# A PSUM tile read by four operations, and the same tile copied out first: one step of a fused forward and backward kernel

## The chip, the cores and the metric

The kernel runs on one core of a Trainium2 chip. The metric is the device time of one execution in microseconds (us): the median of several runs. The engines are PE (TensorE, matrix products out of SBUF into PSUM), DVE (VectorE), ACT (ScalarE), POOL (GpSimd) and SP (SyncE, which here issues DMA transfers). Each engine runs its own instructions in order and waits for others by semaphores.

## The reference

The program computes one block of a speech model (attention beside a gated convolution, merged by a second convolution) and the gradients of all its inputs. B = 2, T = 4000, D = 144, everything in bfloat16. What matters here is the attention and its backward pass:

```
xa  = layernorm(x)
q, k, v = split(xa @ w_qkv)
p   = softmax(q @ k.T / sqrt(D))
attn = p @ v;  glob = attn @ w_att_out
...
out = x + (m + conv(m)) @ w_merge        # m = [glob, loc]
outputs: out and the gradients of x and of all seven weights, for the given grad_out
```

## The kernel before, in words

The projections are folded into small weight products, so that attention works on the normalized input xa itself. For each batch element, `phase_att` goes over 32 tiles of 125 query rows (line 1234, `for t in range(NB + 1)`); the same instructions carry the forward pass and the backward pass of the attention. For tile i:

- `quad` (L1044 to 1056): PE makes scores S and their gradients dP against all 4000 keys, in pieces of 2 x 500 columns. Two PSUM buffers "ps" of 2 x 500 columns hold these pieces in turn; each 500 columns take a main matmul (L1049) and one for the 16 input columns left over (L1055).
- `S_min` (L1072, 1074): DVE copies a score piece, negated, into Pbuf and takes the row minimum; `P_exp` (L1079): ACT turns it into exponentials in place. They stay unnormalized: the row sum comes later, from Y.
- `PdP`: ACT casts a dP piece into Sbuf (L1090) and DVE multiplies it by P (L1092), or DVE does both (L1087).
- `P_tr` (L1082) and `st_half` (L1253): DMA transposes of Pbuf into PT and of Sbuf into ST, issued by SP.
- `Y_half` (L1094 to 1122): Y = P xa, 32 matmuls over the 32 key blocks (L1100), 125 x 145, whose column 144 is the row sum, since xa_aug has a column of ones. Then rl = 1 / row sum (L1106, DVE); dj (L1109, DVE) sums Y times the tile's gradient rows qb into delta; nd = -delta rl (L1111, DVE); yn = Y rl (L1113, ACT), stored to DRAM by SP (L1114); ty = Y nd (L1116, ACT), a term for Z; and QBs (L1118 to 1122, four POOL operations), the rescaled rows that X uses.
- `Z_half` (L1132 to 1144): Z = (P dP) xa by another 32 matmuls (L1138); zn = Z rl + ty (L1142, DVE).
- `X_group` (L1163 to 1183): the key side of the backward pass, X, by matmuls of Sbuf and Pbuf against QBs (L1177), added into acc by DVE (L1183).

Y and Z share one PSUM tile "yz", [125, 2, 145] in f32: one buffer (bufs=1, line 1096 or 1134) holds Z of tile i in its second half and Y of tile i + 1 in its first half. The next such tile is Z of tile i + 1 and Y of tile i + 2, so Z of tile i + 1 can start only when every reader of Y of tile i + 1 is done.

Between the attention steps stand the units of the convolution branch (`local_units`, L421 to 663). Nothing of the order is left to chance: class `Planner` (L666 to 968) takes the program of a phase as a graph, gives each instruction an estimated cost by engine, size and memory (`cost`, L713), starts on each engine the earliest instruction of the program that is ready and has its buffers, and fixes the resulting order on all engines. A new instruction is thus a new node of the graph, and orders elsewhere may change too.

The small tiles come from the pool `small` (L980), with 4 buffers where no number is given.

Of the kernel before, what the change touches and what calls it, by code (L numbers as in the profile page):

```python
# [8 lines left out]
F32 = mybir.dt.float32  # L9
# [7 lines left out]
PB = 125  # L17
# [953 lines left out]
def phase_att(k, W, b, S, A, M, head=None):  # L971
    nc, tc = k.nc, k.tc
# [5 lines left out]
    with ExitStack() as es:  # L978
        ab = es.enter_context(tc.tile_pool(name="att_buf%d" % b, bufs=1, side="left", reuse_waits="tile"))
        small = es.enter_context(tc.tile_pool(name="att_small%d" % b, bufs=4, side="left", reuse_waits="tile"))  # L980
# [113 lines left out]
        def Y_half(i, h):  # L1094
            if h == 0 and i not in YZ:
                yz = ps_yz.tile([PB, 2, 145], F32, tag="yz")
                YZ[i] = yz
            Y = YZ[i][:, 0, :]
            for j in range(16 * h, 16 * h + 16):
                nc.tensor.matmul(Y, PT[0:PB, j, 0:PB], xaa[:, j, 0:D + 1], start=(j == 0), stop=(j == NB - 1))  # L1100
            if h == 0:
                return
            qb = QB.pop(i)
            rl = small.tile([PB, 1], F32, tag="rl")
            RL[i] = rl
            nc.vector.reciprocal(rl[:], Y[:, 144:145])  # L1106
            delta = small.tile([PB, 1], F32, tag="delta")
            dj = small.tile([PB, D], BF, tag="dj", bufs=1)
            nc.vector.scalar_tensor_tensor(dj[:], Y[:, 0:D], rl[:], qb[:, 1, 0:D], op0=ALU.mult, op1=ALU.mult, accum_out=delta[:])  # L1109
            nd = small.tile([PB, 1], F32, tag="nd")  # L1110
            nc.vector.scalar_tensor_tensor(nd[:], delta[:], -1.0, rl[:], op0=ALU.mult, op1=ALU.mult)  # L1111
            yn = small.tile([PB, D], BF, tag="yn", bufs=2)
            nc.scalar.activation(yn[:], Y[:, 0:D], ACT.Copy, scale=rl[:])  # L1113
            nc.sync.dma_start(S.Yn_d[:, i, :], yn[:])  # L1114
            ty = small.tile([PB, D], F32, tag="ty", bufs=2)
            nc.scalar.activation(ty[:], Y[:, 0:D], ACT.Copy, scale=nd[:])  # L1116
            TY[i] = ty
            nc.gpsimd.tensor_scalar(QBs[:, i % NPB, 0, :], qb[:, 0, 0:D], rl[:], 1.0, op0=ALU.mult, op1=ALU.mult)  # L1118
            g0, g1 = (small.tile([PB, D], F32, tag=n_, bufs=1, name=n_) for n_ in ("g0", "g1"))
            nc.gpsimd.tensor_scalar(g1[:], qb[:, 1, 0:D], rl[:], 1.0, op0=ALU.mult, op1=ALU.mult)  # L1120
            nc.gpsimd.tensor_scalar(g0[:], qb[:, 0, 0:D], nd[:], 1.0, op0=ALU.mult, op1=ALU.mult)
            nc.gpsimd.tensor_tensor(QBs[:, i % NPB, 1, :], g0[:], g1[:], op=ALU.add)  # L1122
# [111 lines left out]
        for t in range(NB + 1):  # L1234
# [31 lines left out]
            if head is not None and t < 2:  # L1266
                for s in range(8):
                    for f in steps[8 * t + s]:
                        f()
                    if s < 4:  # L1270
                        S_min(t, s, quad(S_work(t, s), t > 0)[0])
                        if t == 0 and s == 3:
                            for c2 in range(4):
                                P_exp(0, c2)
                    elif t:
                        PdP(0, s - 4, quad(dP_work(0, s - 4))[0], s % 2 == 1)
                for h in range(2 * t):
                    st_half(h)
                    Y_half(0, h)
                if t == 0:  # L1280
                    P_tr(0)
                continue
# [40 lines left out]
            if t < NB:  # L1323
                products(3)
                for h in range(2):
                    if ok(t - 1):
                        Y_half(t - 1, h)
# [11 lines left out]
        for h in range(2):  # L1339
            Y_half(NB - 1, h)  # L1340
# [631 lines left out]
```

## Time and profile before

| | |
|---|---|
| median of 3 runs | 1405.17 us (1404.89 to 1405.4) |
| span of the profiled execution, first to last instruction | 1401.5 us |
| own time of the profiled execution | not listed apart from the span |
| mean granted clock of PE | 0.976 |
| busy: PE, weight loads, DVE, ACT, POOL | 1298.7, 1069.5, 1055.4, 830.5, 541.5 us |
| ACT yn (L1113), ty (L1116), mean of 64 | 372, 375 ns |
| DVE rl (L1106), dj (L1109), nd (L1111), mean of 64 | 161, 361, 180 ns |
| POOL QBs and helpers (L1118, L1120, L1121, L1122), mean of 64 | 397, 414, 401, 508 ns |

The span has a head (0 to 60 us), the attention phase of the first batch element (60 to 660), its merge (to about 760), the attention phase of the second (760 to 1300) and its merge and the final weight gradients. A line of groups or of a timeline names the source line, the engine, the operation and "out<-in" with tile names; "[0.95 <-ACT ty L1116]" means that the engine sat idle for 0.95 us before it and that this ended when ACT finished the instruction of line 1116. In an answer on waits the numbers are the total, the count and the longest.

### The profile page before, as it was taken

The numbers are of one execution on the slowest core, as the hardware profiler recorded it, in microseconds if no ns is written. First come the engines' busy times: TensorE is split into PE (matmuls) and PEld (weight loads), VectorE is DVE, ScalarE is ACT, GpSimd is POOL, SyncE is SP. The second block draws the span as 40 slices with busy tenths as digits, with TensorE's granted clock in tenths as the row PEclk, the third lists the DMA queues.
The fourth block names the chain that finished last, engine by engine and source line by source line (L and its number), as shares of the span: only waits on it lengthen the run. The fifth ranks groups of instructions, "written<-read, shape, count | busy, mean of one in ns | idle before, by whom it ended". The sixth has DMA issues, their size and how long they took to land.

```text
span 1401.5 us, 39725 instructions
## 1 busy us (share of the span) xinstructions
PE 1298.7 (93%) x16254; PEld 1069.5 (76%) x16254; DVE 1055.4 (75%) x2815; ACT 830.5 (59%) x1387; POOL 541.5 (39%) x1087
## 2 busy tenths in 40 slices
PE   5879999999999999998787999999999999999898
PEld 3557877778877877888775778788887787787887
DVE  7368878788887878767737888788888887876564
ACT  4656666666666665553626666666766665565371
POOL 7453333334333333347514334343443433334420
PEclk8899999999999999999998999999999999999999
DMA  4367657757776776785225877767776766866512
GB/s 116 77 106 138 121 107 127 143 108 125 123 125 128 128 128 124 119 175 145 75 54 97 149 129 128 129 127 131 129 135 123 135 126 115 145 122 129 160 42 72
DMA packets 553637, 168.60 MB, mean 120 GB/s; under 512 B 536431, under 2 KB 548353, under 8 KB 553412
## 3 DMA queue, kind: packets, MB, share of 16 engines
q1 hardware_dynamic: 547818, 153.74, 59.5%
q0 software_dynamic: 5088, 12.11, 3.3%
q8 instruction: 127, 2.08, 0.6%
q14 instruction: 56, 0.46, 0.1%
q10 hardware_dynamic: 548, 0.21, 0.1%
HBM read 21.04 MB, written 14.12 MB: 25 GB/s over the span
## 4 chain that ended last, share of the span: by engine, by line
PE 42%; DVE 7%; DMA 7%; ACT 4%; POOL 3%; issue 2%; DVEq 0%; SPq 0%; POOLq 0%; ACTq 0%
PE X L1177 9%; PE ps L1049 7%; PE yz L1138 5%; PE yz L1100 5%; DMA PT<-Pbuf 4%; PE ps L1055 3%; PE po L1525 2%; ACT Pbuf L1079 1%; DMA go_h<-in_grad_out_dram 1%; DVE t L1551 1%; DVE Pbuf L1072 1%; PE pd L564 1%; DMA ST<-Sbuf 1%; DVE acc L1183 1%; PE pc L549 1%
## 5 line engine op out<-in xcount | busy, mean ns | idle before, releaser
L1072 DVE TENSOR_SCALAR_CACHE_REDUCE Pbuf<-ps 125x1000 bf16<-125x1000 f32 x256 | 306.5, 1198 | 119.5 <-PE ps L1055 115.5
L1079 ACT ACTIVATE Pbuf<-Pbuf,nm 125x1000 bf16<-125x1000 bf16 x256 | 283.2, 1135 | 125.8 <-DVE nm L1074 125.7
L1177 PE MATMUL X<-QBs,Sbuf 125*125 125x144 bf16 x2048 | 304.0, 230 | 7.0 <-DVE acc L1183 3.2
L1177 PE MATMUL X<-QBs,Pbuf 125*125 125x144 bf16 x2048 | 300.1, 228 | 4.7 <-POOL QBs L1122 4.7
L1049 PE MATMUL ps<-xaT_m,qt 128*125 128x500 bf16 x1024 | 270.2, 382 | 13.4 <-DVE Pbuf L1072 4.7
L1177 PEld LDWEIGHTS <-Sbuf 125*125 125x125 bf16 x2048 | 264.8, 139 | 20.2 <-issue 20.0
L1177 PEld LDWEIGHTS <-Pbuf 125*125 125x125 bf16 x2048 | 265.6, 139 | 8.5 <-issue 8.2
L1090 ACT CAST Sbuf<-ps 125x1000 bf16<-125x1000 f32 x189 | 187.8, 994 | 139.8 <-PE ps L1055 139.3
L1183 DVE TENSOR_TENSOR acc<-X,acc 125x432 f32<-125x432 f32 x372 | 202.6, 551 | 55.9 <-PE X L1177 53.6
L1138 PE MATMUL yz<-xa_aug,ST 125*125 125x144 bf16 x2048 | 150.1, 229 | 19.4 <-ACT ty L1116 18.3
L1049 PEld LDWEIGHTS <-qt 128*125 128x125 bf16 x1024 | 124.0, 139 | 56.9 <-issue 18.1
L1138 PEld LDWEIGHTS <-ST 125*125 125x125 bf16 x2048 | 141.1, 139 | 26.0 <-issue 24.5
L1100 PE MATMUL yz<-xa_aug,PT 125*125 125x145 bf16 x2048 | 146.4, 229 | 7.3 <-DMA PT<-Pbuf 7.0
L1092 DVE TENSOR_TENSOR Sbuf<-Sbuf,Pbuf 125x1024 bf16<-125x1024 bf16 x189 | 134.3, 711 | 22.4 <-ACT Sbuf L1090 22.1
L1100 PEld LDWEIGHTS <-PT 125*125 125x125 bf16 x2048 | 136.9, 138 | 15.2 <-DMA PT<-Pbuf 10.4
L1055 PEld LDWEIGHTS <-qt 16*125 16x125 bf16 x1024 | 37.1, 129 | 102.9 <-issue 102.9
L1055 PE MATMUL ps<-XR,qt 16*125 16x500 bf16 x1016 | 113.0, 424 | 0.0
L1087 DVE TENSOR_TENSOR Sbuf<-ps,Pbuf 125x1000 bf16<-125x1000 f32 x67 | 80.0, 1194 | 4.6 <-PE ps L1055 2.8
L1118 POOL TENSOR_SCALAR QBs<-qb,rl 125x144 bf16<-125x144 bf16 x64 | 25.4, 397 | 136.9 <-DVE rl L1106 133.2
L597 POOL TENSOR_TENSOR A_dwc<-l_fl,A_dwc 128x512 f32<-128x512 f32 (+2 forms) x48 | 35.5, 740 | 104.3 <-ACT l_fl L596 104.2
L574 POOL TENSOR_SCALAR l_w<-gd,nc,c 125x144 f32<-125x144 bf16 x64 | 30.6, 485 | 87.1 <-DVE nm L1074 44.7
L1152 ACT COPY zt<-pt 128x250 bf16<-128x250 bf16 x64 | 23.7, 370 | 66.6 <-PE pt L1150 66.4
(557 smaller groups left out, 2562.5 us busy)
## 6 DMA issues: line engine op xcount, KB each, us to landing
Yn_d<-yn SPq DMA_DIRECT2D x64, 35.2 KB
Zn_d<-zn SPq DMA_DIRECT2D x64, 35.2 KB
ug_d<-ugr SPq DMA_DIRECT2D x32, 70.3 KB
xo<-in_x_dram SPq DMA_DIRECT2D x16, 140.6 KB
out_dram<-dxo SPq DMA_DIRECT2D x16, 140.6 KB
go_h<-in_grad_out_dram POOLq DMA_DIRECT2D x4, 504.0 KB, 6.7
Zn<-Zn_d SPq DMA_DIRECT2D x4, 504.0 KB
ST<-Sbuf SPq DMA_TRANSPOSE x124
```

The costliest lines, as they stand in the source:

```text
L597: nc.gpsimd.tensor_tensor(acc, fl[0:rows, 0:n], acc, op=ALU.add)
L1049: mm = nc.tensor.matmul(pp[r // 2][:, r % 2, 0:CH], QT[i][:, 3 * h, :], xaTm[:, c * CH:(c + 1) * CH], start=True, stop=False)
L1055: nc.tensor.matmul(pp[r // 2][:, r % 2, 0:CH], QT[i][rs, 1 + (q // 2 + h) % 2, :], xr, start=False, stop=True)
L1072: nc.vector.tensor_scalar(pv(Pbuf, i % NPB, c2), src, -1.0, 3.0e38, op0=ALU.mult, op1=ALU.min, accum_out=NM[i][:, c2:c2 + 1])
L1079: nc.scalar.activation(v, v, ACT.Exp, bias=NM[i][:, 4:5], scale=-1.0)
L1087: nc.vector.tensor_tensor(pv(Sbuf, i % NDB, c2), src, pv(Pbuf, i % NPB, c2), op=ALU.mult)
L1090: nc.scalar.copy(pv(Sbuf, i % NDB, c2), src)
L1092: nc.vector.tensor_tensor(sc, sc, pchunk(i % NPB, c2), op=ALU.mult)
L1100: nc.tensor.matmul(Y, PT[0:PB, j, 0:PB], xaa[:, j, 0:D + 1], start=(j == 0), stop=(j == NB - 1))
L1138: nc.tensor.matmul(Z, ST[0:PB, j, 0:PB], xaa[:, j, 0:D], start=(j == 0), stop=(j == NB - 1))
L1177: nc.tensor.matmul(X[:, jj, :], l, r, start=(n_ == 0), stop=(n_ == len(ops) - 1))
L1183: nc.vector.tensor_tensor(av, X[:, 0:nj, :], av, op=ALU.add)
```

## The change

After the last Y matmul of a tile, ACT copies all 145 columns of Y out of PSUM into a new SBUF tile ys (f32, two buffers), and the name Y then stands for that copy: rl, dj, yn and ty read ys. Nothing else differs in the source.

```
--- before.py
+++ after.py
@@ -1101,6 +1101,9 @@
             if h == 0:
                 return
             qb = QB.pop(i)
+            ys = small.tile([PB, 145], F32, tag="ys", bufs=2)
+            nc.scalar.copy(ys[:], Y)
+            Y = ys
             rl = small.tile([PB, 1], F32, tag="rl")
             RL[i] = rl
             nc.vector.reciprocal(rl[:], Y[:, 144:145])
```

Lines after 1103 of the old program are three lines further down in the new one: yn, L1113 before, is L1116 after, and ty, L1116 before, is L1119 after.

More of the change, by code (lines that the diff above doesn't have):

```diff
@@ L1103, in Y_half @@
             qb = QB.pop(i)
+            ys = small.tile([PB, 145], F32, tag="ys", bufs=2)
+            nc.scalar.copy(ys[:], Y)
+            Y = ys
             rl = small.tile([PB, 1], F32, tag="rl")
```

## The prediction

> **What bounds the kernel now.** I read the busy shares first, then the stages, then what TensorE (PE) waits for in the two long stages, then one such wait instruction by instruction.
>
> The page's first part gives PE 93% of the span, VectorE (DVE) 75%, ScalarE (ACT) 59%. The stretches of time show where this holds (columns: length, then PE, weight loads, DVE, ACT and POOL busy, granted clock, DMA share, GB/s):
>
> ```profile
> 60.00:660.00 600.00, 566.73 (x7106) 466.84 (x7107) 465.57 (x1209) 361.29 (x578) 243.66 (x494) 0.98 0.70 128
> ...
> 760.00:1300.00 540.00, 521.20 (x6580) 426.42 (x6580) 434.11 (x1076) 339.86 (x545) 204.39 (x413) 1.00 0.73 132
> ```
>
> These are the attention phases of the two batch elements. PE is idle for 33.3 us of the first and 18.8 us of the second; no other engine is above 80%. PE runs its instructions in a fixed order, so nearly every idle microsecond of PE there is time lost. The waits of PE in the two stretches name the causes:
>
> ```profile
> PE yz L1138 <- ACT ty L1116: 12.4, 12, 2.3
> PE yz L1100 <- DMA PT<-Pbuf: 2.7, 6, 0.8
> PE X L1177 <- DVE acc L1183: 2.5, 5, 0.9
> ...
> PE X L1177 <- POOL QBs L1122: 2.0, 3, 1.6
> ```
>
> ```profile
> PE yz L1138 <- ACT ty L1116: 6.0, 5, 2.6
> PE yz L1100 <- DMA PT<-Pbuf: 4.3, 5, 1.1
> ...
> PE X L1177 <- POOL QBs L1122: 1.1, 1, 1.1
> ```
>
> The reader sees one leading cause: the matmuls of Z (L1138) wait 12.4 + 6.0 = 18.3 us (17 times; unrounded) for the ACT operation that makes ty (L1116), the last reader of Y in the one PSUM buffer that Y and Z share. One such wait, with start, length, engine and line:
>
> ```profile
> 217.31 0.80 PE L1100 MATMUL yz<-xa_aug,PT 125*125 125x145 bf16 x10
> ...
> 218.14 0.17 DVE L1106 RECIPROCAL rl<-yz 125x1 f32<-125x1 f32 x1 [0.55 <-PE yz L1100]
> ...
> 218.35 0.37 DVE L1109 SCALAR_TENSOR_TENSOR dj<-yz,rl,qb 125x144 bf16<-125x144 f32 x1
> 218.41 0.38 POOL L1118 TENSOR_SCALAR QBs<-qb,rl 125x144 bf16<-125x144 bf16 x1 [2.98 <-DVE rl L1106]
> ...
> 218.75 0.38 ACT L1113 ACTIVATE yn<-yz,rl 125x144 bf16<-125x144 f32 x1
> 218.75 0.20 DVE L1111 SCALAR_TENSOR_TENSOR nd<-delta,rl 125x1 f32<-125x1 f32 x1
> ...
> 219.67 0.39 ACT L1116 ACTIVATE ty<-yz,nd 125x144 f32<-125x144 f32 x1
> ...
> 220.10 1.30 PE L1138 MATMUL yz<-xa_aug,ST 125*125 125x144 bf16 x18 [0.95 <-ACT ty L1116]
> ```
>
> From the end of Y to Z there are five steps on two engines (rl, dj, nd, yn, ty), each behind other work in its queue: 2.2 us, of which PE could fill about 1.2.
>
> **What the change does, part by part.** A copy of the whole Y by ACT stands ahead of rl; rl, dj, yn and ty read the copy. PE's instructions are the same in number, but a planner orders each engine by its own costs, so I compared the two programs' orders, counting PE's work between two points in columns at 0.42 ns (the chain gives four 500-column matmuls 0.85 us).
>
> *Moved: Z.* Before, the work that PE has between the last Y matmul and the first Z matmul is 3.4 us on average; after, 2.6 us. Before, 13 tiles have 1.4 us or less there, and all 13 are among the 17 that wait: 16.2 of the 18.3 us. After, 26 tiles have 1.4 us or less, but what they need is shorter.
>
> *Removed:* the wait for ty, **-18.3 us**.
>
> *Added: Z waits for the copy.* The price of the copy: the nearest row is the PSUM to SBUF f32 copy of 80x144 (l_fl, L596), 272 ns; the 128x250 copy (zt) takes 370 ns. I take 0.28 us. In the tile above PE goes on to the next matmuls at 217.94 and rl starts at 218.14, 0.20 us later; at another wait Z starts 0.06 us after ty ends (504.81 + 0.38 to 505.25). So Y to Z is 0.20 + 0.28 + 0.06 = 0.54 us if ACT is free. With ACT always free only tile 1 (no work between) and one other wait, 0.6 us in all: the lower end. The upper end is as much as now, 18.3. ACT is busy 60 to 63% of these stretches with operations of 0.62 us on average (361.29 over 578), the longest 1.1; being in the middle of one costs 0.6 x 0.4 = 0.25 us on average, against 0.56 us of slack in the commonest case (1.1 less 0.54). In seven of the close tiles the exponential of 1.1 us stands right ahead of the copy, in most of the others work that is ready 4 us before. I take 0.15 us for each of 26 tiles, nearer to the lower end because the chain has one queue in place of two: **+4 us**.
>
> *Added: rl, nd and QBs come later* by the copy and a hand-over, 0.34 us. PE needs QBs in X (L1177). Before, X waits 3.1 us for it in the two stretches (above). The chain from Y to the second QBs is 0.20 + 0.34 + 0.17 + 0.37 + 0.08 + 0.20 + 0.39 + 0.49 and some 0.3 of hand-overs, 2.5 us, and up to 1.2 more behind a row minimum (L1072) on DVE. In the new order 8 tiles have 3.1 us of PE work or less before their first X, and no wait of Z now stretches it. Lower end 0, upper end 8 x 1.2 = 9.6; I take 0.4 each, **+3 us**.
>
> *Added: ACT's work.* 64 x 0.28 = 18 us for the copy. yn and ty read SBUF instead of PSUM: the exponential (SBUF, one pointer) takes 1135 ns at 1000 columns, the cast (PSUM, none) 994, and a pointer costs 372 - 272 = 100 ns (yn against l_fl), which leaves about 40 ns for SBUF; 128 x 0.04 = 5 us. dj reads SBUF too: two-tensor DVE operations of 144 columns take 300 ns with a PSUM input (L568) and 299 without (L1540), so nothing. 23 us on an engine with 40% idle lie beside PE's work, but what stands behind the copy comes 0.36 us later: the casts that free the score buffers, qb, qt, zt. PE's waits for ACT other than ty are 5.5 us in the two stretches; by a third more, **+2 us** (ends 0 and 6). Cover gone, it would be the 23 us.
>
> *What is late next.* With Z earlier, ST must be there (0.9 us of waits now) and the next Y still needs the transpose PT (7.0 us now); DMA is at 0.70 to 0.73 and does not get faster. **+1 us**, ends 0 and 7. SP issues the same transfers; the store of yn leaves a little later and nobody reads it in the phase. The new tile is 580 bytes a partition, twice, and starts no transfer.
>
> Sum: -18.3 + 4 + 3 + 2 + 1 = -8.3 us on the profiled execution, whose span is 1401.5 us. The page has no other time of that execution; the median of the runs is 3.7 us above the span, and I carry that over: 1405.2 - 8.3 = **1397 us**.
>
> One rule weighs against the change. The trace first: POOL's L1118 starts 0.06 us after rl together with dj, and L1120, 0.38 us in the timeline above, took 0.65 us in another tile while DVE ran two operations with both inputs in SBUF (L581, L523). The Trainium skill, "SBUF — State Buffer", "Who interferes with whom", says that a DVE instruction with two SBUF inputs holds up a GpSimd instruction that reads SBUF. By it dj, which now reads the copy and qb, would hold up every first QBs by up to its own 0.3 us, and the term for QBs would be 8 x 0.3 = 2.4 us larger, 1399 us.
>
> **The rivals.** Faster or slower means by over 0.2%, 2.8 us, about what a measurement of this kernel can tell from no change.
>
> 1. *The whole wait goes.* ACT is free whenever Y ends and nothing else is late: -18.3 + 0.6, 1387.5 us. For it: the copy's predecessors are mostly long ready. Against: ACT is 60% busy, and idle PE rarely vanishes without a remainder.
> 2. *The stall moves.* Y waits for PT, or quads for their score buffers, by as much as Z gains; the upper ends above (7 + 6) nearly do it: 1403 to 1407 us. For it: the chain that ended last runs through 8.8 us of PT transfer ahead of one Y (530.34 to 539.15). Against: in the order, the last score quad lies 18.5 us of PE work before its Y, after as before (18.7).
> 3. *QBs becomes the bound.* If POOL is held up as in the trace's 0.65 us row and the copy adds its 0.34, QBs is 0.6 us later; 17 tiles have 4.3 us or less before X: 17 x 0.6 = 10 us, and the sum is +1.7 us, 1407. This is what the page's rule would lead to where it bites hardest.
> 4. *Slower: rl blocks DVE.* rl waits for ACT at the head of DVE's queue, and the minima and products behind it (L1072, L1087), which free the score buffers for PE, wait with it. DVE is 78 to 80% busy. If the 0.34 us of each of 64 tiles reaches PE in full, it costs 21.8 us: -18.3 + 4 + 21.8 = +7.5, 1413 us. It decides once more than 14.3/64 = 0.22 us a tile reaches PE. For it: rl already waits 22.2 us for Y (22 times). Against: DVE waits 115.5 us for score quads at L1072, so it is mostly ahead of PE.
>
> That the change does nothing is excluded: in the new order the copy is the only reader of Y in PSUM, and Z stands earlier.
>
> **How the numbers follow.** Forecast (1392 to 1402): 0.48. Rival 1: 0.14. Rival 2: 0.12. Rival 3: 0.06. Rival 4: 0.20, half of it above 1412, since a new plan can also misplace work that I have not priced. Faster: 0.48 + 0.14 = 0.62; same: 0.12 + 0.06 = 0.18; slower: 0.20. The range 1387 to 1412 reaches from rival 1 to rival 4 and leaves out 0.05 below and 0.10 above. The likeliest case's own range is 1392 to 1402.
>
> **What would show it.** Waits of Z for ty are gone and those for the copy are under 8 us; the copy's row is near 0.28 us, yn and ty near 0.41; X's waits for QBs are near 6 us; PE's idle time in the two stretches falls from 52 to about 44 us. I am wrong if Z waits for the copy as long as for ty (ACT's queue is the fault), if L1049 or L1100 takes over the idle time (rivals 4 and 2), or if X does (rival 3).

## The result, and the profile after

| | before | after |
|---|---|---|
| median | 1405.17 us (1404.89 to 1407.62, 5 runs) | 1409.72 us (1408.88 to 1413.59, 5 runs) |
| span of the profiled execution | 1401.5 us | 1407.1 us |
| PE busy, idle | 1298.7, 102.8 us | 1301.9, 105.2 us |
| first rl to last rl, both attention phases | 1101.7 us | 1107.1 us |
| ACT, POOL busy | 830.5, 541.5 us | 847.6, 554.4 us |

The ratio is 1.0038, 95% interval 1.0023 to 1.0054: 5 us slower, where 8 us faster was forecast. All of it lies in the attention phases (+5.4 us); head, middle and tail together stay within 0.3 us. (The time between the first and the last rl of a phase is used below as "the phases"; a profiled span alone would mix in the final stage.) The accounts by waits below are of one execution of each kernel. Single executions of the kernel before lay between 1402.5 and 1413.6 us in the later runs, so a piece of 1 or 2 us in such an account shows little by itself.

The two long stretches after, with the columns of before (length, then PE, weight loads, DVE, ACT, POOL, clock, DMA share, GB/s):

```profile
60.00:660.00 600.00, 565.98 (x7074) 465.66 (x7073) 464.61 (x1198) 369.11 (x610) 250.96 (x497) 0.98 0.71 128
760.00:1300.00 540.00, 517.90 (x6501) 421.19 (x6501) 434.31 (x1077) 349.21 (x579) 210.15 (x414) 1.00 0.73 129
```

PE gets fewer matmuls done in the same 1140 us (13,575 against 13,686) and is idle for 56.1 us of them instead of 52.1. What it waits for, in the whole run, after:

```profile
PE yz L1100 <- DMA PT<-Pbuf: 12.9, 16, 2.1
PE X L1180 <- POOL QBs L1125: 11.1, 13, 1.6
...
PE pt L588 <- ACT zt L1155: 2.9, 5, 0.7
```

and before:

```profile
PE yz L1138 <- ACT ty L1116: 18.3, 17, 2.6
...
PE yz L1100 <- DMA PT<-Pbuf: 7.0, 11, 1.1
...
PE X L1177 <- POOL QBs L1122: 4.7, 5, 1.6
```

The wait that the change was to remove is gone: Z waits for ty no more, and for the copy once, 0.4 us. But three others have grown. Summed over the printed rows of each releaser: PT +5.9 us, QBs +6.6, ACT's other results +7.3 (zt alone 1.5 to 7.1), all else +1.1. That is -18.3 + 0.4 + 5.9 + 6.6 + 7.3 + 1.1 = +3.0 us. PE's idle time by the page grows by 2.4 us; the rest of the span's +5.6 us is PE's busy time, +3.2 us for the same 16,254 matmuls, spread over the groups with no more than 2.2 us in one. Most of that is waiting too. Matmuls overlap: a Y matmul is listed with 229 ns, but ten in a row took 0.80 us in the tile of the prediction, one about every 0.06 us, so the first 0.17 us or so of every wait still counts as busy. In the phases PE stands idle before 93 matmuls instead of 80. At these places its busy time beyond the usual distance of two such matmuls (the median in the kernel before) is 18.7 us instead of 15.4.

The tile shown in the prediction, in the timeline after:

```profile
219.87 3.58 PE L1100 MATMUL yz<-xa_aug,PT 125*125 125x145 bf16 x32 [2.12 <-DMA PT<-Pbuf]
223.49 0.28 ACT L1105 COPY ys<-yz 125x145 f32<-125x145 f32 x1 [2.92 <-PE yz L1100]
...
223.81 0.16 DVE L1109 RECIPROCAL rl<-ys 125x1 f32<-125x1 f32 x1 [3.48 <-ACT ys L1105]
...
224.34 0.86 PE L1141 MATMUL yz<-xa_aug,ST 125*125 125x144 bf16 x11
```

Where Z began 0.95 us late behind ty, it now starts 0.57 us after the copy's end with no wait. But Y itself began 2.12 us late, for its transpose PT, and ACT stood idle for 2.92 us at the copy: its order is fixed, and the copy at the head of its queue waits for the last Y matmul. What ACT waits for in the whole run, after and then before:

```profile
ACT ys L1105 <- PE yz L1100: 102.9, 40, 5.5
ACT Pbuf L1079 <- DVE nm L1074: 60.9, 34, 4.2
```

```profile
ACT Pbuf L1079 <- DVE nm L1074: 125.7, 49, 5.5
```

ACT used to stand at the exponential until the row minimum nm was there; now it stands for 103 us at the copy, with the exponentials behind it. In ACT's order the copy is ahead of 177 of the 252 exponentials of the next tile; before, yn was the first ACT operation on Y, and it was ahead of 98. One such place after, and the same tile before:

```profile
1039.94 0.15 DVE L1074 TENSOR_REDUCE nm<-nm 125x1 f32<-125x4 f32 x1
...
1040.85 0.28 ACT L1105 COPY ys<-yz 125x145 f32<-125x145 f32 x1 [5.27 <-PE yz L1100]
1041.02 3.17 ACT L1079 ACTIVATE Pbuf<-Pbuf,nm 125x1000 bf16<-125x1000 bf16 x3
```

```profile
1031.84 0.15 DVE L1074 TENSOR_REDUCE nm<-nm 125x1 f32<-125x4 f32 x1
1032.02 3.17 ACT L1079 ACTIVATE Pbuf<-Pbuf,nm 125x1000 bf16<-125x1000 bf16 x3 [3.72 <-DVE nm L1074]
```

Before, the exponentials start 0.03 us after nm; after, 0.93 us. Over all 64 row minima this lag is 9.8 us before and 19.8 us after. The copy also stands between the four exponentials of a tile: from nm to the end of the last of them it is 495.2 us before and 518.5 us after, again summed over the 64 tiles. Every exponential sits ahead of a PT transpose, and PT is what Y then waits for.

### The profile page after: what moved, and what is told of

Its sections match the earlier page's. It is cut to its first block, busy times and chain, and to the rows that moved or that the text cites. A ratio compares the mean times of both kernels' runs of the same rounds, so it can differ in the third digit from the quotient of the medians.

```text
span 1407.1 us, 39740 instructions
## 1 busy us (share of the span) xinstructions
PE 1301.9 (93%) x16254; PEld 1071.5 (76%) x16254; DVE 1058.1 (75%) x2815; ACT 847.6 (60%) x1451; POOL 554.4 (39%) x1087
## 4 chain that ended last, share of the span: by engine, by line
PE 59%; DMA 14%; DVE 11%; ACT 8%; POOL 5%; issue 3%; SPq 0%; ACTq 0%; POOLq 0%; DVEq 0%
PE X L1180 13%; PE ps L1049 11%; DMA PT<-Pbuf 9%; PE yz L1100 7%; PE yz L1141 6%; PE ps L1055 5%; ACT Pbuf L1079 3%; PE po L1528 3%; DVE Pbuf L1072 2%; DMA ST<-Sbuf 2%; DVE acc L1186 1%; DMA go_h<-in_grad_out_dram 1%; ACT Sbuf L1090 1%; DVE t L1554 1%; PE pc L549 1%
## 5 line engine op out<-in xcount | busy, mean ns | idle before, releaser
L1180 PE MATMUL X<-QBs,Pbuf 125*125 125x144 bf16 x2048 | 300.5, 228 | 11.1 <-POOL QBs L1125 11.1
L1049 PE MATMUL ps<-xaT_m,qt 128*125 128x500 bf16 x1024 | 268.6, 381 | 12.1 <-DVE Pbuf L1072 4.8
L1180 PEld LDWEIGHTS <-Pbuf 125*125 125x125 bf16 x2048 | 265.8, 139 | 10.4 <-issue 9.8
L1121 POOL TENSOR_SCALAR QBs<-qb,rl 125x144 bf16<-125x144 bf16 x64 | 32.3, 505 | 150.5 <-DVE rl L1109 145.6
L1105 ACT COPY ys<-yz 125x145 f32<-125x145 f32 x64 | 17.8, 279 | 103.3 <-PE yz L1100 102.9
```

The lines of the kernel that those rows point to most:

```text
L1049: mm = nc.tensor.matmul(pp[r // 2][:, r % 2, 0:CH], QT[i][:, 3 * h, :], xaTm[:, c * CH:(c + 1) * CH], start=True, stop=False)
L1180: nc.tensor.matmul(X[:, jj, :], l, r, start=(n_ == 0), stop=(n_ == len(ops) - 1))
```

## The experiments

Ratios are to the kernel before, run on the same chip (medians 1406.8 to 1407.3 us). Three theories stood at the start: **A**, the copy at the head of ACT's queue holds up what is behind it; **B**, rl and QBs come later, and POOL is held up by dj; **C**, the planner found another order and that order lost what the release gained.

**Parts of the change, each with the order that the planner gives it.**

e1_plan_held keeps the change's operations but tells the planner that yz is occupied until ty, as before:

```
+            elif o[0].split("_")[0] == "ty" and i_[0] in src:
+                uses[src[i_[0]]].add(g)
+                keep[g] = {src[i_[0]]}
...
```

> The operations of the changed kernel, but the planner is told that the shared PSUM tile is held until ty, as before the change, so that Z is not planned earlier (mean PE work between Y and Z 3.46 us as before, against 2.70 in the changed kernel). Theory A (the copy blocks ACT's queue, and exponentials and zt behind it come late): the copy still stands in ACT's order at Y's planned end, 1407 to 1411 us. Theory B (QBs late, by the copy ahead of rl and by dj holding up POOL): 1407 to 1411 us. Theory C (the new plan spends the gain: Z stands right behind its release and other dependences become tight): the wait for ty goes and little else changes, 1392 to 1399 us.

1416.97 us, 1.0074 [1.0058, 1.0090]; phases 1114.1 us; above the ranges of all three theories. It is slower than the change, so planning Z early was not what lost: C in this form fell. The waits for PT (18.0) and QBs (9.8) are there without it. (Each of these edits also gives the planner another program, and so another order; what that does by itself is measured further down.)

e4_ty_psum lets ty read PSUM again, so that it holds the buffer:

```
-            nc.scalar.activation(ty[:], Y[:, 0:D], ACT.Copy, scale=nd[:])
+            nc.scalar.activation(ty[:], YZ[i][:, 0, 0:D], ACT.Copy, scale=nd[:])
```

> As the changed kernel, but ty alone still reads Y in PSUM, so that Z waits for ty as before; rl, dj and yn read the copy. PE's order is instruction by instruction that of the run with the held plan, so the two differ only in whether Z really waits for ty. If freeing the tile is worth what the waits say, this one is 12 to 18 us slower than the held plan under every theory; against before it shows the bare cost of the copy: A and B 1415 to 1425 us, C 1406 to 1411 us.

1421.85 us, 1.0099 [1.0083, 1.0115]. Z waits 23.5 us for ty again. The order is that of e1 on all engines but for a few instructions, so the release by itself is worth 1421.85 - 1416.97 = 4.9 us here, less than the 12 to 18 expected and far less than the 23.5 us of waits that it takes away: most of that comes back in other waits (PT is 18.0 us in e1 and 11.7 in e4). The profiled execution of e4, from which its waits are, took 1430.1 us, the longest of its five.

e2_dj_psum lets dj read PSUM, so that it has one SBUF input:

```
-            nc.vector.scalar_tensor_tensor(dj[:], Y[:, 0:D], rl[:], qb[:, 1, 0:D], op0=ALU.mult, op1=ALU.mult, accum_out=delta[:])
+            nc.vector.scalar_tensor_tensor(dj[:], YZ[i][:, 0, 0:D], rl[:], qb[:, 1, 0:D], op0=ALU.mult, op1=ALU.mult, accum_out=delta[:])
```

> As the changed kernel, but dj alone reads Y in PSUM, so it has one SBUF input; Z then waits for the copy and for dj. Theory B: POOL's first QBs operation falls from 505 ns to about 400, X's waits for QBs fall from 11.1 us to about 7, 1400 to 1405 us. Theory A: no change in the waits for PT (12.9 us), 1407 to 1411 us. Theory C: the plan has Z later again (mean 3.3 us), 1398 to 1405 us, with PT and QBs waits both nearer to before.

1414.14 us, 1.0050 [1.0038, 1.0062], above the ranges of all three theories. POOL's first QBs operation falls from 505 to 405 ns and X's waits for QBs from 11.1 to 6.3 us, as B has it, but PT rises to 16.5 us, and the time does not fall. POOL's hold-up is real and, as far as one other order can tell, not the main cause.

e3_dve_copy moves the copy to DVE:

```
-            nc.scalar.copy(ys[:], Y)
+            nc.vector.tensor_copy(ys[:], Y)
```

> As the changed kernel, but DVE makes the copy. ACT no longer stands at the copy waiting for Y. Theory A: the waits for PT fall from 12.9 us to 8 or less and those for zt from 7 to 2, 1396 to 1403 us, less what 18 us more of DVE work cost. Theory B: dj still has two SBUF inputs and QBs is as late, 1407 to 1412 us, waits for QBs near 11 us. Theory C: another plan, Z at 3.5 us behind Y, 1397 to 1405 us.

1398.67 us, 0.9933 [0.9916, 0.9949]; phases 1095.8, in the range of A and in that of C. ACT waits for nm 125.3 us as before, the lag of the exponentials is 9.1 us, PT 10.5 (A had 8 or less). The release is the same, and the last QBs of a tile ends 3.92 us after Y as in the change (3.91; 3.50 before). So it is not these two that set the change apart from e3, but ACT's queue or the order.

e5_copy_alone keeps ACT's copy, but nobody reads it:

```
-            Y = ys
```

> The kernel before plus the ACT copy, which nothing reads: rl, dj, yn and ty read PSUM, Z waits for ty, POOL is not held up. In ACT's order the copy stands ahead of 170 of the 252 exponentials of the following tile, against 177 in the changed kernel; yn, the first to wait for Y before, stands ahead of 98. Theory A (ACT's queue): 1416 to 1424 us, waits for PT well above 7 us, waits of the exponential for nm near 60 us in place of 126. Theory B (QBs by dj and POOL): 1405 to 1411 us. If the copy's 18 us lay beside other work as predicted: 1404 to 1409 us.

1423.79 us, 1.0129 [1.0112, 1.0146]; phases 1120.4: the 17.8 us of copies on an engine with 40% idle time come with phases 18.7 us longer, the new order included. This is A's expectation. ACT stands 72.2 us before a copy that is used for nothing, until Y is there, and 18.1 us more for which the view names no releaser, and PT reaches 15.4 us.

**The copy placed later.** e6_copy_late has the planner believe that the matmuls of Y, and of Z, end 1.5 us later, so that ACT comes to the copy when Y is there; n3_before_late is the same edit in the kernel before.

```
+                if g["e"] == "PE" and g["t"].startswith("yz"):
+                    end += 1.5
```

> The changed kernel with one line in the planner: results of the yz matmuls count as 1.5 us later, so the copy stands later in ACT's order, ahead of 133 exponentials of the following tile in place of 177. Theory A: ACT waits at the copy for less than 70 us in place of 102.9, waits for PT below 12.9, 1398 to 1406 us. Theory B: dj still has two SBUF inputs, 1407 to 1412 us.

> Control for the run with the copy planned later: the kernel before with the same line in the planner; the operations are those of before. Theory A: ACT's order is hardly touched (yn ahead of 79 exponentials in place of 98), within 5 us of before. If the plan alone decides and not the copy, this gains or loses as much as the other.

e6: 1416.72 us, 1.0075 [1.0060, 1.0089]; n3: 1411.53 us, 1.0042 [1.0025, 1.0059]. In e6 ACT stands only 11.6 us at the copy, the lag of the exponentials is back at 9.5 us, from nm to the end of the last one it is 495.1 us as before, and PT is at 10.0; but rl now starts 2.04 us after Y (0.75 in the change), and X waits 19.3 us for QBs, Z 6.6 for ST. It is no faster, so A's expectation was missed (and B's, which ended at 1412): the stall at the copy is gone, and a later rl has taken its place. In the kernel before, the same edit costs 0.42% by itself; against this twin e6 is 0.33% slower, much as the change is against before.

**The order held.** e7_same_plan plans as before, with ys counted as yz, and puts each copy into ACT's order at rl's planned start; e8_same_plan_dve puts it on DVE right ahead of rl; f1_alone_same_plan is e7 with readers left on PSUM (no `Y = ys`).

```
+        todo = [i for i in self.nc.cur_bb.bb.instructions[i0:i1] if i.name not in own]
...
+                at = next((n for n, h in enumerate(order[e]) if times[h] >= times[g] - 1e-9), len(order[e]))
...
+                order[e].insert(at, len(groups) - 1)
```

> The operations of the changed kernel in the order of the kernel before: the planner plans the program without the copies, reading ys as yz, and each copy is then put into ACT's order at the planned start of its rl. Within the planned phases the order of all five engines is that of before, so only the copy and its consequences differ. Theory A (the copy at the head of ACT's queue holds up the exponentials behind it): 1411 to 1420 us, exponentials wait for nm near 60 us in place of 126. Theory C in its new form (the copy is cheap and frees Z, and only the new order lost the gain): 1388 to 1397 us.

> As the run with the copies in the old order, but DVE makes the copy, right ahead of rl. ACT's order in the planned phases is that of before, with nothing added. Theory A: the wait for ty is gone at the price of 20 us of DVE work, 1390 to 1400 us. If the gain of the first DVE run came from its new order: 1403 to 1411 us.

> The kernel before with the ACT copy that nothing reads, in the order of before: Z waits for ty, rl waits for the copy. Against the full change in the same order (1405.0 us) it lacks only the reading of the copy and so the early release. If the copy costs what the release saves by the waits, 18 us: 1419 to 1426 us. If the release is worth only the 5 to 10 us by which the held plan beat its twin: 1410 to 1416 us.

| | median | ratio | phases |
|---|---|---|---|
| f1, copy alone on ACT | 1418.72 us | 1.0079 [1.0058, 1.0100] | 1114.9 us |
| e7, the change on ACT | 1405.02 us | 0.9992 [0.9980, 1.0003] | 1101.8 us |
| e8, the change on DVE | 1402.09 us | 0.9969 [0.9958, 0.9980] | 1098.7 us |

All three fell between the two ranges that had been set for them. The order of the other instructions is that of before within each planned phase, so this is the cleanest account. The copy alone costs 1114.9 - 1101.7 = 13.2 us; reading it, which frees yz, gives back 1114.9 - 1101.8 = 13.1; the sum is nothing. (By the medians it is 11.1 and 12.2 us.) Since PE's order is the same, its distances from matmul to matmul can be compared with those of before one by one. In f1 Y takes 4.4 us more, Z 2.6, X 4.7 and all else 1.2. In e7 Z takes 19.4 us less, so the release is worth its full price there; but X takes 11.2 us more (8.1 of it at waits for QBs), Y 3.7 and all else 4.5. Waits of PE in f1 and in e7:

```profile
PE yz L1159 <- ACT ty L1137: 21.6, 17, 2.7
PE yz L1119 <- DMA PT<-Pbuf: 10.1, 12, 2.1
PE X L1198 <- POOL QBs L1143: 7.8, 9, 1.6
```

```profile
PE X L1199 <- POOL QBs L1144: 11.2, 12, 1.6
PE yz L1119 <- DMA PT<-Pbuf: 10.3, 12, 1.4
```

In f1 all three waits are some 3 us longer than before. The first exponential of a tile is hardly later here (lag 12.1 us), but from nm to the end of the last one it is 508.0 us (507.5 in e7) instead of 495.2, so ACT's queue delays PT in this order too. What is also later is rl. DVE's wait for it, 22.2 us before, is in f1:

```profile
DVE rl L1127 <- ACT ys L1124: 57.1, 56, 7.5
```

From the end of Y to rl's start it is 0.93 us on average in f1 and e7, 0.38 before. That is the wait that rival 4 described; how much of the 13 us comes by DVE's queue, how much by QBs and how much by the exponentials the runs do not tell apart. With the copy on DVE (e8) rl starts 0.71 us after Y, the last QBs ends after 3.75 us instead of 3.96, X waits 6.1 us for QBs instead of 11.2, and the phases are 3.1 us shorter than e7's.

**Other orders of the same three programs.** One cost of the planner is changed by a trifle: each matmul 0.3 ns longer (`+ 0.0015` to `+ 0.0018`) or each ACT operation 5 ns longer (`0.17` to `0.175`), in the kernel before (n1, n2), in the change (a1, a2) and in the DVE copy (d1, d2).

> The kernel before, but the planner counts each matmul 0.3 ns longer: the same operations in another order (a sixth of PE's order differs), yn ahead of 100 exponentials. It shows how much a new plan alone moves the time. Theory A: within 3 us of before. If any new plan can do what the change did, 4 us or more to either side.

> The kernel before with another constant of the planner (each ACT operation counted 5 ns longer): a third order of the same operations. From the two other new orders of before: 1408 to 1413 us; if the first two were unlucky, 1402 to 1407.

> The changed kernel with matmuls counted 0.3 ns longer by the planner, the twin of the kernel before with the same line (1410.8 us). If the change costs the same under another plan, 1413 to 1417 us; if its +0.4% was the luck of one order, anything from 1402 to 1411 us.

> The changed kernel with the same constant. If the copy on ACT is neutral apart from the order, as in the order of before: within 4 us of its twin of before, to either side. If it is a loss of its own: 4 to 10 us above it.

> The DVE copy with matmuls counted 0.3 ns longer by the planner, the third of these twins. Theory A: about 8 us below the twin of before again, 1400 to 1405 us. If the first DVE run had a lucky order: 1406 to 1414 us.

> The DVE copy with the same constant. If the DVE copy is a gain of its own, as in three orders so far: 5 to 17 us below its twin of before, 1393 to 1404 us. If those were luck: 1405 or more.

| planner's costs | before | copy on ACT | copy on DVE |
|---|---|---|---|
| as they are | 1.0000 (1405.17 us) | 1.0038 [1.0023, 1.0054] | 0.9933 [0.9916, 0.9949] |
| matmul + 0.3 ns | 1.0038 [1.0023, 1.0053] | 1.0005 [0.9992, 1.0018] | 0.9920 [0.9896, 0.9944] |
| ACT + 5 ns | 0.9950 [0.9931, 0.9969] | 1.0021 [1.0003, 1.0039] | 0.9989 [0.9973, 1.0004] |
| mean | 0.9996 | 1.0021 | 0.9947 |

A new order alone moves the unchanged program from -0.50% to +0.38% (+0.42% in n3), as much as the change did. Against its twin in the same row the copy on ACT is at +0.38, -0.33 and +0.71%, the copy on DVE at -0.67, -1.18 and +0.39%; a2 is 10.4 us above n2, where 4 to 10 had been set as the sign of a loss, and n2 itself came out below both of its ranges. Of the change's +0.38% one can therefore say that the mechanism gives nothing or a small loss, not that it is 5 us. n1's phases are those of before (1101.9 us), and 3.3 of the 5.2 us that its span is longer lie in the tail (104.3 us against 101.0); n2's phases are 5.5 us shorter. The fastest is d1_dve_plan_pe, 1393.91 us (1392.52 to 1401.64), ahead of both kernels and below both of its ranges; of its gain the order may be as large a part as the engine.

Across all kernels one pattern holds. Where ACT copies and the planner puts the copy where it likes (after, e1, e2, e4, e5, a1, a2) the lag of the exponentials is 16.8 to 21.5 us and PT costs PE 10.7 to 18.0 us, 14.4 on average. In the others (before, n1 to n3, e3, e6 to e8, f1, d1, d2) the lag is 6.9 to 12.1 us and PT costs 7.0 to 10.5, 9.3 on average. So A is a part of the change's cost, about 5 us of PT by this comparison, in which the orders differ too, and not the whole.

## Why the prediction was wrong

**The release: right, and better than forecast.** The wait of 18.3 us went in full (with the order held, Z takes 19.4 us less), and the copy, put at +4 us, cost Z 0.4 us. ACT was free when Y ended, because the planner had left it standing there; I counted that as a gain of Z's and not as a loss for the rest of ACT.

**The step that failed** is "23 us on an engine with 40% idle lie beside PE's work", at +2 us, and with it "what is late next", at +1. The copies cost ACT what was expected (279 ns each, forecast 0.28 us; yn 410 and ty 408 ns, forecast 0.41 us). What was missed is where the operation stands: I counted what stands behind the copy as 0.36 us late, named casts, qb, qt and zt, and left out the exponentials. The order that I had before me showed the copy ahead of 177 of them. ACT's idle time was not free time, it was the time in which it waited for nm; it now waits for Y in its stead. Measured: ACT's other results +7.3 us (forecast +2), PT +5.9 and ST +0.3 (forecast +1 for both). That the work did not lie beside PE's is shown with the order held: the same copies, read by nobody, made the phases 13.2 us longer (f1), the later rl included.

**QBs: the delay was right, the size off.** The forecast delay was 0.34 us at +3 us. From Y's end to rl's start it grew from 0.38 to 0.75 us, to the end of the last QBs from 3.50 to 3.91. X pays 6.6 us for it instead of +3 (with the order held, X takes 11.2 us more, the largest piece of what Z's gain went into): it waits 13 times, not 8, and POOL's first QBs operation is longer too:

```profile
L1121 POOL TENSOR_SCALAR QBs<-qb,rl 125x144 bf16<-125x144 bf16 x64 | 32.3, 505 | 150.5 <-DVE rl L1109 145.6
```

It was 397 ns before. The Trainium skill, "SBUF — State Buffer", "Who interferes with whom", has a DVE instruction with two SBUF inputs hold up a GpSimd instruction that reads SBUF; the trace agrees, +108 ns here and +8 ns in e2, where dj reads PSUM. By that rule the term was put at 2.4 us more; e2's waits for QBs are 4.8 us shorter, in another order. (The prediction has the first QBs operation 0.06 us after rl; in the rows of before it is 0.10 us after rl's end, with dj. No term hangs on it.)

**The rivals.** Rival 2 named PT, which took 5.9 us, without the cause. Rival 3's hold-up is confirmed, as a part; its sum had the copy's 0.34 us twice, in the +3 and in the 0.6: with 10 in place of 3 it is -18.3 + 4 + 10 + 2 + 1 = -1.3 us, 1404 instead of 1407. Rival 4's wait is there in the held order (f1), where rl's wait at the head of DVE's queue goes from 22.2 to 57.1 us; in the change itself DVE waits for rl as long as before, 22.3 us, since the planner moved rl behind other work (35.7 us of it in all between Y's end and rl, 27.0 before). The prediction excluded that the change does nothing; with the order held, e7's 0.9992 [0.9980, 1.0003] cannot be told from nothing.

**The sum.** -18.3 + 4 + 3 + 2 + 1 = -8.3 was forecast. By the profile it is -18.3 + 0.4 + 6.6 + 7.3 + 5.9 + 1.1 = +3.0, and 5.6 with what else the span grew. The prediction had a new plan that "can also misplace work" only inside rival 4; n1 and n2 show -0.50% to +0.38% from the order alone, which belonged beside the sum as a case of its own.

**Not settled:** what part of the 13 us of the held copy comes through rl and QBs and what part through the later exponentials; which feature of an order makes the 0.5%; and how much of d1's gain the DVE copy would keep in yet another order, since in the third (d2 against n2) it lost.

## What to carry to other kernels

Here the copy that freed a PSUM buffer early removed the whole wait and gained nothing, since what stood behind it in the queue, and what came later because of it, fed the next waits. Before placing such a copy, read the order of the copying engine, not its busy share, and ask what it waited for in its idle time. Where a planner makes the order, run the unchanged program in two or three other orders first; a difference below theirs says nothing about the change. Price each later link of a chain, even one of 0.4 us, at every place where the consumer has no slack.

## What the runs showed of the hardware

ACT's read of the PSUM tile never overlapped DVE's read of it. Before, yn started 0.04 us or more after dj's end and never less than 0.44 us after rl's; after, with both in SBUF, yn starts as early as 0.03 us after rl. In f1, rl takes nothing from the copy and still waits for it 56 times, as shown above. The Trainium skill, "PSUM — Partial Sum Buffer", "PSUM bank collisions raise a hardware error", says that the compiler's scheduler orders accesses of the same 32 partitions of one bank by two engines, reads too; the trace agrees with an order, and no run here shows an overlap. So several readers of one PSUM tile on two engines form a chain, which a copy cuts to one link.

Reading SBUF costs ACT more: yn and ty took 410 and 408 ns where they took 372 and 375 ns out of PSUM. For DVE, dj went from 361 to 389 ns, where the forecast had nothing. The same copy took 279 ns on ACT and 304 ns on DVE.
